# One table sets the order of every engine up to the third token group, in a recurrent attention followed by a gated MLP

## The chip, the cores and the metric

The kernel runs on one core of a Trainium2 chip. A core has a matrix engine (TensorE, PE in the profile), a vector engine (VectorE, DVE), a scalar engine (ScalarE, ACT), GpSimd (POOL) and SyncE (SP), which here only issues transfers. Each engine works through its own queue in order. The metric is the time of one execution in microseconds on the device; lower is better.

## The reference

For each of 4 batches and 8 heads a recurrence runs over 768 positions with head dimension 48. Its output, 3072 tokens of 384 features, goes through a gated MLP with 1536 hidden features.

```python
for t in range(S):
    kt, vt, rt, wt = k[:, :, t], v[:, :, t], r[:, :, t], w[:, :, t]
    cur = np.einsum('bhd,bhe->bhde', u[None] * kt, vt)
    y[:, :, t] = np.einsum('bhd,bhde->bhe', rt, state + cur)
    state = wt[:, :, :, None] * state + np.einsum('bhd,bhe->bhde', kt, vt)
x = y.transpose(0, 2, 1, 3).reshape(B * S, H * D)
g = x @ w_gate
out = (g * (1 / (1 + np.exp(-g))) * (x @ w_val)) @ w_out      # w_*: float64
```

r, k, v, w and u are float32; the three weight matrices arrive as float64.

## The kernel before

**Chunks.** The recurrence is done in 24 chunks of 128 positions, six for each batch, all eight heads at once (four pairs of heads, the halves of a pair on partitions 0 to 47 and 64 to 111). For a chunk n, VectorE scans the decays backwards (`qt`, L192), takes the reciprocal of the whole chunk's decay (L196, L197), multiplies k by it (`kq`, L198), scans forwards (`et`, L201) and multiplies r (L202). From k, r and u in natural order it makes the diagonal term `a0` (L211 to L214), which ScalarE spreads over an identity (`at`, L231). TensorE turns k around (`kb`, L239), multiplies the scores (`sc`, L253); VectorE puts the scores below the diagonal into `at` by a mask (L255). TensorE then forms the chunk's state (`dl`, L272; added to the decayed old state by VectorE, `st` and `sp`) and the output `y` (L301), which ScalarE and VectorE split into an upper half `xh` and a remainder `xl` (L308, L309). In the code a chunk is three steps of a generator, each followed by a third of the preparation of chunk n+1.

**Groups.** The 24 chunks are the tokens of seven groups of 4, 2, 4, 4, 4, 4 and 2 chunks. For a group the MLP runs over twelve blocks f of hidden features: two halves `gv` of nine matmuls each (gate and value; three products of halves for each of three slices of x, L385), SiLU on ScalarE (`sg`, L392), the product on VectorE (L393), its upper half and remainder (`hh` L395, `hl` L397), and the output product `po` (L406), which is issued one block late. After the last block ScalarE copies the output out of PSUM (`ob`, L417) and SyncE stores it.

**Weights.** Block f's weights come as pairs of 32-bit words and are converted once, during the start and group 0: two passes on ScalarE (L150, L152), three on VectorE (L154, L155, L157), the upper half on ScalarE (L158) and the remainder on VectorE (L159). Two blocks' raw weights fit at a time; the load of block f+2 is issued when block f is converted.

**Buffers.** PSUM's eight banks are two buffers for `kb`, `sc`, `dl` and `y` (the pool psA), two for `gv`, four for `po`. In SBUF two buffers take turns for each of the loads `kr` (k and r), `ws` (decays) and `vt` (v), one for `nat`; chunks 2 and 3 keep their kr in buffers that later hold group 1's x.

**Order.** TensorE's instructions run in the order in which the code lists them: the start (chunks 0 to 3, with spin matmuls on a constant between the steps), and then the groups' blocks, with the next group's chunk steps between them at fixed blocks (`at_block`). The transfers of the start are in the code's order too. Everything else on VectorE, ScalarE and SyncE is ordered by the scheduler of the framework. In group 0 the conversion of block f+2 is held behind the one before it.

Of the kernel before, what the change touches and what calls it, by code (L numbers as in the profile page):

```python
# [9 lines left out]
F32 = mybir.dt.float32  # L10
F32R = mybir.dt.float32r
# [25 lines left out]
PEND_MIN = 1e-15  # L37

# [10 lines left out]
def recurrence_then_glu_kernel(  # L49
# [30 lines left out]
    xs, raws, masked = {}, {}, [None]  # L80
# [53 lines left out]
    w_l = cpool.tile([P, NF, 3, DM], F32R, tag="w_l", name="w_l")  # L134

    def load_weights(f):
        raw = wst.tile([P, 3, DM, 2], I32, tag="raw", name=f"raw_{f}")
        for i, src in enumerate((gv_d[f, 0], gv_d[f, 1], wo_d[f])):
            queue(nc.sync.dma_start(raw[:, i].rearrange("p c t -> p (c t)"), src.bitcast(I32)))
        return raw  # L140

    def convert(f):

        raw = raws.pop(f)
        top, low = raw[:, :, :, 1], raw[:, :, :, 0]
        hi, lo = w_h[:, f], w_l[:, f]


        tf, tu = top.bitcast(F32), top.bitcast(U32)
        nc.scalar.activation(tf, tf, AF.Copy, scale=2.0**-112)  # L150

        nc.scalar.activation(low, low.bitcast(U32), AF.Copy, scale=2.0**-29)  # L152
        s = wst.tile([P, 3, DM], U32, tag="s", name=f"s_{f}", bufs=1)
        nc.vector.tensor_scalar(s, tu, 0x1FFFFFFF, 3, ALU.bitwise_and, ALU.logical_shift_left)  # L154
# [3 lines left out]
        nc.scalar.activation(hi, af, AF.Copy)  # L158
        last = nc.vector.tensor_tensor(lo, af, hi.bitcast(F32), ALU.subtract)  # L159
# [5 lines left out]
    wss, krs, nats, vts = {}, {}, {}, {}

    def load_ws(n):
        wss[n] = ld.tile([PR, L + 1], F32, tag="ws", name=f"ws_{n}")
        queue(nc.sync.dma_start(wss[n], wt_d[n]))

    def load_kr(n):

        pool, tag = {2: (mp, "xh"), 3: (mp, "xl")}.get(n, (ld, "kr"))
        krs[n] = pool.tile([PR, 2, NPR, C], F32, tag=tag, name=f"kr_{n}")
        queue(nc.sync.dma_start(krs[n], kr_d[n]))

    def load_nat(n):
        nats[n] = ld.tile([P, 2, H, D], F32, tag="nat", name=f"nat_{n}", bufs=1)
        queue(nc.sync.dma_start(nats[n], nat_d[n]))

    def load_vt(n):
        vts[n] = ld.tile([P, H, D], F32, tag="vt", name=f"vt_{n}")
        queue(nc.sync.dma_start(vts[n], v_d[n]))

    state = [None]

    def prepare(n):

        ws, kr, vt = wss.pop(n), krs[n], vts[n]
        kq, re = kr[:, 0], kr[:, 1]  # L190
        qt = ap_.tile([PR, NPR, C + 1], F32, tag="qt", name=f"qt_{n}", bufs=1)
        nc.vector.tensor_tensor_scan(  # L192
            _flat(qt)[:, ::-1], ws[:, 1:][:, ::-1], _flat(d1q)[:, ::-1], 0.0, ALU.mult, ALU.add
        )
        nc.scalar.activation(pend[:, n, :], qt[:, :, 0], AF.Copy)
        nc.vector.tensor_scalar(d1e[:, :, 0], qt[:, :, 0], PEND_MIN, None, ALU.max)  # L196
        nc.vector.reciprocal(d1e[:, :, 0], d1e[:, :, 0])  # L197
        nc.vector.tensor_tensor(kq, kq, qt[:, :, 1:], ALU.mult)  # L198
# [12 lines left out]
        nc.vector.tensor_tensor(ru, ru, u_bc, ALU.mult)  # L211
        nc.vector.tensor_tensor(ru, ru, nat[:, 0], ALU.mult)
        a0 = ap_.tile([P, H], F32, tag="a0", name=f"a0_{n}")
        nc.vector.tensor_reduce(a0, ru, AX.X, ALU.add)  # L214
        if n + 1 < NC:
            load_nat(n + 1)

        vz = vzs[n % 2]
        vp = vt.rearrange("s (p j) e -> s p j e", j=2)
        nc.scalar.activation(vz[:, :, 0, : D - 32], vp[:, :, 0, 32:], AF.Copy)  # L220
        nc.scalar.activation(vz[:, :, 1, D - 32 :], vp[:, :, 1, : 64 - D], AF.Copy)
        yield a0, vz

    def diagonals(n, a0):

        at = []
        for j in range(2):
            a = ap_.tile([P, NPR, C], F32, tag="at", name=f"at_{n}_{j}", bufs=3)
            for p in range(NPR):
                h = 2 * p + j  # L230
                nc.scalar.activation(a[:, p, :], ident, AF.Copy, scale=a0[:, h : h + 1])  # L231
# [12 lines left out]
    def scores(n, kq, re, at):

        c = n % NCH
        sc = [psA.tile([P, NPR, C], F32, tag="pa", name=f"sc_{n}_{j}") for j in range(2)]
        for p in range(NPR):
            for j in range(2):
                o = slice(64 * j, 64 * j + D)  # L250
                for m in range(2):
                    ms = slice(64 * m, 64 * m + 64)
                    pin(nc.tensor.matmul(sc[j][ms, p, :], kq[o, p, ms], re[o, p, :], start=True, stop=True))  # L253
        for j in range(2):
            masked[0] = nc.vector.copy_predicated(at[j], mask4, sc[j])  # L255
# [353 lines left out]
```

## Time and profile before

| | |
|---|---|
| median of 3 runs | 627.27 us (623.29 to 627.89) |
| the profiled execution | 626.31 us |
| its span, first to last instruction | 624.6 us |
| TensorE, VectorE, ScalarE busy | 579.5, 356.1, 265.5 us |
| mean granted clock of TensorE | 0.972 |
| first product of group 0, 1, 2 | 60.91, 164.41, 224.78 us |
| last matmul of the last group ends | 617.4 us |

A row of the timeline has the start (us from the span's start), the duration, engine, line, operation, tile written <- tiles read, and in brackets the idle time of the engine before it and what ended that. A row of the stages has the stretch, its length, each engine's busy time with its count of instructions, the granted clock of TensorE (1.00 is full), the busy share of the DMA engines and GB/s. A group of instructions by line has its count, the busy time, the mean ns of one, and the idle time before them with what ended most of it. L numbers are lines of the kernel before.

### The profile page before, as it was taken

How to read it: one execution, taken by the hardware profiler on the slowest of the kernel's cores; microseconds unless marked ns; L12 is line 12 of the kernel's file. 1: busy time of each engine (PE TensorE's matmuls, PEld its weight loads, DVE VectorE, ACT ScalarE, POOL GpSimd, SP SyncE). 2: the span in 40 equal slices, each digit the busy share in tenths (PEclk: the TensorE clock that was granted, in tenths of full speed). 3: DMA queues.
4: the chain of work that ended last, by engine and by line, in shares of the span. 5: the costliest groups of instructions: out<-in, count | busy, mean ns of one | idle time of the engine just before them, and what ended most of it. 6: DMA issues, size and time to landing. Idle time of an engine off the chain costs nothing.

```text
span 624.6 us, 12577 instructions
## 1 busy us (share of the span) xinstructions
PE 579.5 (93%) x5330; PEld 501.0 (80%) x5330; DVE 356.1 (57%) x595; ACT 265.5 (43%) x609; POOL 1.9 (0%) x11
## 2 busy tenths in 40 slices
PE   7688999476989989999999999999999999999995
PEld 5477788364889978888888888888888888888994
DVE  7984789978567766365456556545644533132221
ACT  5646666743544444334345333443533432121321
POOL 1000000000000000000000000000000000000000
PEclk9888999979989999999999999999999999999998
DMA  9646453423332233211212212221210110000100
GB/s 276 196 149 181 168 173 126 167 84 95 93 96 83 85 108 83 68 45 54 70 67 83 69 23 76 84 85 50 84 43 1 43 51 2 1 1 0 52 1 30
DMA packets 21903, 50.67 MB, mean 81 GB/s; under 512 B 2513, under 2 KB 8785, under 8 KB 21841
## 3 DMA queue, kind: packets, MB, share of 16 engines
q1 hardware_dynamic: 21840, 49.81, 25.6%
q8 instruction: 44, 0.72, 0.5%
q14 instruction: 19, 0.15, 0.1%
HBM read 45.08 MB, written 4.72 MB: 80 GB/s over the span
## 4 chain that ended last, share of the span: by engine, by line
PE 71%; DVE 10%; DMA 8%; ACT 5%; issue 3%; SPq 1%; DVEq 0%; ACTq 0%
PE gv L385 40%; PE po L406 21%; DMA raw<-in_wo_dram 5%; PE y L301 5%; PE sc L253 3%; DMA vt<-in_vn_dram 2%; DVE qt L192 2%; ACT w_h L158 1%; DVE s L155 1%; PE dl L272 1%; ACT raw L152 1%; DVE s L157 1%; DVE et L201 1%; PE kb L239 1%; ACT at L231 1%
## 5 line engine op out<-in xcount | busy, mean ns | idle before, releaser
L385 PE MATMUL gv<-xh,w_h 128*128 128x512 f32 (+1 forms) x504 | 184.1, 365 | 3.1 <-DVE sg L393 1.8
L385 PE MATMUL gv<-xh,w_l 128*128 128x512 f32 (+1 forms) x504 | 181.6, 360 | 1.0 <-DVE w_l L159 1.0
L385 PE MATMUL gv<-xl,w_h 128*128 128x512 f32 (+1 forms) x504 | 182.2, 361 | 0.0
L393 DVE TENSOR_TENSOR sg<-sg,gv 128x512 f32<-128x512 f32 (+1 forms) x84 | 51.0, 607 | 146.4 <-PE gv L385 145.0
L385 PEld LDWEIGHTS gv<-xh,w_h 128*128 128x128 f32 x504 | 95.0, 189 | 17.6 <-DVE sg L393 3.0
L385 PEld LDWEIGHTS gv<-xl,w_h 128*128 128x128 f32 x504 | 95.0, 188 | 15.3
L385 PEld LDWEIGHTS gv<-xh,w_l 128*128 128x128 f32 x504 | 95.0, 189 | 14.1 <-DVE w_l L159 1.3
L406 PE MATMUL po<-w_h,hh 128*128 128x384 f32 x288 | 101.1, 351 | 0.5 <-ACT hh L395 0.5
L406 PE MATMUL po<-w_h,hl 128*128 128x384 f32 x288 | 97.7, 339 | 2.4 <-DVE hl L397 2.4
L406 PE MATMUL po<-w_l,hh 128*128 128x384 f32 x288 | 97.3, 338 | 0.0
L395 ACT ACTIVATE hh<-sg 128x512 fp32r<-128x512 f32 (+1 forms) x84 | 47.8, 569 | 110.1 <-DVE sg L393 110.1
L392 ACT ACTIVATE sg<-gv 128x512 f32<-128x512 f32 (+1 forms) x84 | 44.7, 533 | 111.8 <-PE gv L385 106.5
L397 DVE TENSOR_TENSOR hl<-sg,hh 128x512 fp32r<-128x512 f32 (+1 forms) x84 | 51.6, 614 | 36.6 <-ACT hh L395 36.0
L231 ACT ACTIVATE at<-ident,a 128x128 f32<-128x128 f32 x192 | 60.7, 390 | 14.3 <-PE y L301 9.3
L406 PEld LDWEIGHTS po<-w_h,hh 128*128 128x128 f32 x288 | 54.3, 189 | 9.0 <-issue 6.0
L406 PEld LDWEIGHTS po<-w_h,hl 128*128 128x128 f32 x288 | 54.3, 189 | 4.6 <-DVE hl L397 3.2
L406 PEld LDWEIGHTS po<-w_l,hh 128*128 128x128 f32 x288 | 54.4, 189 | 0.0
L255 DVE COPY_PREDICATED at<-mask,sc 128x512 f32<-128x512 uint32 x48 | 32.5, 728 | 8.1 <-PE sc L253 8.1
L253 PE MATMUL sc<-kr 48*64 48x128 f32 x768 | 30.8, 279 | 6.9 <-DVE xl L309 3.8
L253 PEld LDWEIGHTS sc<-kr 48*64 48x64 f32 x768 | 22.8, 134 | 15.5 <-issue 4.9
L198 DVE TENSOR_TENSOR kr<-kr,qt 112x512 f32<-112x512 f32 x24 | 16.5, 689 | 29.7 <-DMA kr<-in_kr_dram 29.7
L204 ACT ACTIVATE ws<-ws 112x517 f32<-112x517 f32 x24 | 15.3, 636 | 42.8 <-DVE et L201 42.7
(64 smaller groups left out, 564.0 us busy)
## 6 DMA issues: line engine op xcount, KB each, us to landing
kr<-in_kr_dram SPq DMA_DIRECT2D x24, 448.0 KB, 4.0
nat<-in_nat_dram SPq DMA_DIRECT2D x24, 384.0 KB, 3.1
raw<-in_gv_dram SPq DMA_DIRECT2D x24, 384.0 KB, 4.0
ws<-in_wt_dram SPq DMA_DIRECT2D x24, 226.2 KB, 2.6
vt<-in_vn_dram SPq DMA_DIRECT2D x24, 192.0 KB, 3.5
raw<-in_wo_dram SPq DMA_DIRECT2D x12, 384.0 KB, 4.8
out_dram<-ob SPq DMA_DIRECT2D x24, 192.0 KB, 1.8
u_bc<-in_u_dram SPq DMA_DIRECT2D x1, 192.0 KB, 4.8
```

The source lines that it names most:

```text
L198: nc.vector.tensor_tensor(kq, kq, qt[:, :, 1:], ALU.mult)
L204: nc.scalar.activation(ws, ws, AF.Square)
L231: nc.scalar.activation(a[:, p, :], ident, AF.Copy, scale=a0[:, h : h + 1])
L253: pin(nc.tensor.matmul(sc[j][ms, p, :], kq[o, p, ms], re[o, p, :], start=True, stop=True))
L255: masked[0] = nc.vector.copy_predicated(at[j], mask4, sc[j])
L301: pin(nc.tensor.matmul(y[32 * g : 32 * g + 32, b // 4, :], lhs, rhs, start=first[g] == i, stop=last[g] == i,))
L385: pin(nc.tensor.matmul(gv, a[:, f, j, q * P : (q + 1) * P], x[:, q, :], start=m == 0, stop=m == 3 * NK - 1,))
L392: nc.scalar.activation(sg, ps[0], AF.Silu)
L393: nc.vector.tensor_tensor(sg, sg, ps[1], ALU.mult)
L395: nc.scalar.activation(hh, sg, AF.Copy)
L397: nc.vector.tensor_tensor(hl, sg, hh.bitcast(F32), ALU.subtract)
L406: pin(nc.tensor.matmul(po[j], a[:, ts], x[:, f, 2, :], start=f == 0 and i == 0, stop=f == NF - 1 and i == 2,))
```

## The change

The code of the start and of groups 0 and 1, with all chunk steps up to the output of chunk 9 (the last of group 2), is now one table of some 700 entries. Each entry names a step and its indices (`pred:4:0` is the mask of chunk 4's even heads, `gv:0:2:1` the value half of block 2 of group 0, `spin:22` that many spin matmuls). The code walks the table and calls the steps; while it does so, the instructions of VectorE, ScalarE, TensorE and the transfers all keep the table's order on their engines. From group 2 on the blocks and chunk steps follow as before by `at_block`, and the scheduler orders VectorE, ScalarE and SyncE as before. What else differs:

- the scores of chunks 0 to 3 are in the four banks of `po`, no more in psA; from chunk 4 on they are in psA;
- a SiLU of one element on ScalarE at the very start, so that its table of functions is loaded there and not in group 0;
- the shared 16 columns of v are copied to a padded tile by one ScalarE instruction for a chunk, no more by two;
- the reciprocal of the chunk's decay is taken without the maximum before it (L196); a chunk for which that matters is sent to the fallback by the same test as before;
- 223 spin matmuls in place of 216;
- from group 2 on, the output product `po` stands behind the chunk's `kb`, no more ahead of it, in three of a group's blocks.

```diff
+FREE = 2
+ORDER = """
+spin:25 ws:0 nat:0 ub:0 kr:0 ws:1 raw:0 scan:0 vt:0 seed:0 kr:1 whole:0 raw:1 ru:0 ruk:0 vt:1 a0:0
...
+hh:1:11 hl:1:11
+"""
...
+    def keep(ins):
+        if early[0]:
+            tc.keep_in_program_order(ins)
...
+    nc.scalar.activation(warm, warm, AF.Silu)
...
+    def seed(n):
+        keep(nc.vector.reciprocal(d1e[:, :, 0], qts[n][:, :, 0]))
...
-        nc.scalar.activation(vz[:, :, 0, : D - 32], vp[:, :, 0, 32:], AF.Copy)
-        nc.scalar.activation(vz[:, :, 1, D - 32 :], vp[:, :, 1, : 64 - D], AF.Copy)
+        keep(nc.scalar.activation(z[:, :, ::2, :], shared.rearrange("s p (j e) -> s p j e", j=2), AF.Copy))
...
-        sc = [psA.tile([P, NPR, C], F32, tag="pa", name=f"sc_{n}_{j}") for j in range(2)]
+        if n < first:
+            scs[n] = [psM.tile([P, NPR, C], F32, tag="po", name=f"sc_{n}_{j}", bufs=4) for j in range(2)]
+        else:
+            scs[n] = [psA.tile([P, NPR, C], F32, tag="pa", name=f"sc_{n}_{j}") for j in range(2)]
...
+    for item in ORDER.split():
+        name, *at = item.split(":")
+        ops[name](*map(int, at))
     early[0] = False
...
+    for g in range(FREE, len(GROUPS)):
         steps = 3 * GROUPS[g + 1] if g + 1 < len(GROUPS) else 0
         at_block = [k * (NF - 1) // steps for k in range(steps)]
...
         for f in range(NF):
+            block(g, f)
+            for k in range(at_block.count(f)):
+                if k == 0 and f == 0:
+                    behind()
+                    waiting = None
+                next(attention)
+            if waiting:
+                behind()
+            waiting = (g, f)
```

**Chunk 4's scores on TensorE.** Before (sc_4 are the scores, dl_4 the state products, y_4 the output of chunk 4; gv_0_8_1 is the value half of block 8 of group 0):

```order
L385 MATMUL gv_0_8_1_1278<-xl_0_176,w_h_100 128x512
L253 MATMUL sc_4_0_1295<-kr_4_632 64x128 x2
L253 MATMUL sc_4_1_1296<-kr_4_632 64x128 x2
...
L272 MATMUL dl_4_1324<-vt_4_634,kn_4_1242 32x48
L272 MATMUL dl_4_1324<-vt_4_634,kn_4_1242 16x48
...
L301 MATMUL y_4_1344<-kr_4_632,sp_89 32x128 x12
```

and now:

```order
L483 MATMUL gv_0_2_1_963<-xl_0_319,w_h_103 128x512
L338 MATMUL sc_4_0_983<-kr_4_325 64x128 x2
L338 MATMUL sc_4_1_984<-kr_4_325 64x128 x2
...
L517 MATMUL po_0_0_918<-w_h_103,hh_0_1_974 128x384
...
L483 MATMUL gv_0_3_0_1022<-xh_0_318,w_h_103 128x512
...
L483 MATMUL gv_0_3_1_1037<-xh_0_318,w_h_103 128x512
...
L483 MATMUL gv_0_4_0_1083<-xh_0_318,w_h_103 128x512
...
L358 MATMUL dl_4_1100<-vt_4_691,kn_4_907 32x48
```

The scores moved from block 8 to block 2, and between them and the state products now stand two output products and three halves of the MLP.

**The mask of chunk 4 on VectorE**, with what stands ahead of it. Before (s_10 and w_l_101 belong to the conversion of block 10, qt_5 to chunk 5's preparation, at_4 is the masked tile):

```order
L397 TENSOR_TENSOR hl_0_8_1293<-sg_0_8_1288,hh_0_8_1291 128x512
L154 TENSOR_SCALAR s_10_1262<-raw_10_1143 128x1152
L196 TENSOR_SCALAR d1e_87<-qt_5_1254 112x4
L198 TENSOR_TENSOR kr_5_794<-kr_5_794,qt_5_1254 112x512
L155 SCALAR_TENSOR_TENSOR s_10_1262<-raw_10_1143,s_10_1262 128x1152
L197 RECIPROCAL d1e_87<-d1e_87 112x4
L157 ISA s_10_1262<-raw_10_1143,s_10_1262 128x2304
L159 TENSOR_TENSOR w_l_101<-s_10_1262,w_h_100 128x1152
L255 COPY_PREDICATED at_4_0_1244<-mask_81,sc_4_0_1295 128x512
L255 COPY_PREDICATED at_4_1_1249<-mask_81,sc_4_1_1296 128x512
```

and now:

```order
L282 TENSOR_TENSOR kr_4_325<-kr_4_325,et_4_847 112x512
L295 TENSOR_TENSOR nat_5_939<-nat_5_939 128x384
L221 TENSOR_TENSOR w_l_104<-s_4_911,w_h_103 128x1152
L505 TENSOR_TENSOR hl_0_1_1001<-sg_0_1_913,hh_0_1_974 128x512
L207 TENSOR_SCALAR s_5_1003<-raw_5_868 128x1152
L343 COPY_PREDICATED at_4_0_934<-mask_81,sc_4_0_983 128x512
L211 SCALAR_TENSOR_TENSOR s_5_1003<-raw_5_868,s_5_1003 128x1152
L495 TENSOR_TENSOR sg_0_2_1005<-sg_0_2_1005,gv_0_2_1_963 128x512
```

The mask stands inside a conversion, one step of it ahead, and the mask of the other half comes later (behind hl_0_4, in the conversion of block 7).

**The end of group 1 on VectorE.** st_9, sp_89 and xl_2 belong to chunk 9, kr_11 and et_11 to chunk 11's preparation, sg_1_* and hl_1_* to the last blocks of group 1. Before:

```order
L393 TENSOR_TENSOR sg_1_10_2367<-sg_1_10_2367,gv_1_10_1_2357 128x256
L281 TENSOR_TENSOR st_9_2391<-dl_9_2374,sp_89 48x192 x2
L397 TENSOR_TENSOR hl_1_10_2372<-sg_1_10_2367,hh_1_10_2370 128x256
L260 TENSOR_TENSOR sp_89<-st_9_2391,pend_99 48x4x48 x2
L214 TENSOR_REDUCE a0_12_2862<-nat_12_2655 128x8
L198 TENSOR_TENSOR kr_11_2425<-kr_11_2425,qt_11_2534 112x512
L309 TENSOR_TENSOR xl_2_1664<-y_9_2394,xh_2_1663 128x3x128
L201 SCALAR_TENSOR_TENSOR et_11_2562<-ws_11_2125,d1e_87 112x516
L393 TENSOR_TENSOR sg_1_11_2463<-sg_1_11_2463,gv_1_11_1_2453 128x256
```

and now:

```order
L495 TENSOR_TENSOR sg_1_7_2260<-sg_1_7_2260,gv_1_7_1_2262 128x256
L369 TENSOR_TENSOR st_9_2319<-dl_9_2272,sp_89 48x192 x2
L505 TENSOR_TENSOR hl_1_7_2324<-sg_1_7_2260,hh_1_7_2322 128x256
L349 TENSOR_TENSOR sp_89<-st_9_2319,pend_102 48x4x48 x2
L299 TENSOR_REDUCE a0_12_2847<-nat_12_2642 128x8
L271 TENSOR_TENSOR kr_11_2333<-kr_11_2333,qt_11_2520 112x512
L408 TENSOR_TENSOR xl_2_1735<-y_9_2290,xh_2_1734 128x3x128
L276 SCALAR_TENSOR_TENSOR et_11_2547<-ws_11_2116,d1e_87 112x516
L495 TENSOR_TENSOR sg_1_8_2358<-sg_1_8_2358,gv_1_8_1_2348 128x256
```

The same sequence now stands between blocks 7 and 8, so that the last four blocks of group 1 run behind the last chunk step.

On SP's queue the start's transfers are now ws_0, nat_0, u_bc, kr_0, ws_1, the three of raw_0, vt_0, kr_1, the three of raw_1; before they were ws_0, kr_0, nat_0, u_bc, vt_0, ws_1, kr_1, vt_1 and then raw_0.

More of the change, by code (lines that the diff above doesn't have):

```diff
@@ L165, in recurrence_then_glu_kernel @@
[L165 to L177 removed]
+            keep(nc.sync.dma_start(raws[f][:, i].rearrange("p c t -> p (c t)"), src.bitcast(I32)))
@@ L400, in output, with prepare, attention_steps @@
-    def output(po, f, hh, hl, name):
-        for j in range(len(po)):
+    def prepare(n):
+        for op in (scan, whole, seed, kq):
+            op(n)
+        yield
+        for op in (scan2, re, check):
+            op(n)
+        if n + 2 < NC:
+            ws(n + 2)
+        yield
+        for op in (ru, ruk, a0):
+            op(n)
+        if n + 1 < NC:
+            nat(n + 1)
+        vz(n)
+        yield
+    def attention_steps(start):
+        for n in range(start, NC):
+            c = n % NCH
+            ahead = prepare(n + 1) if n + 1 < NC else iter([0] * 3)
+            if c < NCH - 1:
+                kb(n)
+                kn(n)
+            for j in range(2):
+                diag(n, j)
+            next(ahead)
+            yield
+            sc(n)
+            for j in range(2):
+                pred(n, j)
+            if c > 0:
+                spb(n)
+            next(ahead)
+            yield
+            if c < NCH - 1:
+                dl(n)
+                st(n)
+            y(n)
+            xh(n)
+            xl(n)
+            if n + 2 < NC:
+                kr(n + 2)
+                vt(n + 2)
+            next(ahead)
+            yield
@@ new lines, in recurrence_then_glu_kernel, with gv @@
+    gvs, sgs, hhs, hls, pos = {}, {}, {}, {}, {}
+    def gv(g, f, j):
+        x_h, x_l = xs[g]
+        nt = x_h.shape[2]
+        ps = psM.tile([P, nt], F32, tag="gv", name=f"gv_{g}_{f}_{j}", bufs=2)
+        m = 0
+        for q in range(NK):
+            for a, x in ((w_h, x_h), (w_l, x_h), (w_h, x_l)):
+                pin(nc.tensor.matmul(
+                    ps, a[:, f, j, q * P : (q + 1) * P], x[:, q, :], start=m == 0, stop=m == 3 * NK - 1,
+                ))
+                m += 1
+        gvs[g, f, j] = ps
@@ L428, in spin @@
         for _ in range(times):
-            pin(nc.tensor.matmul(idle, mask.bitcast(mybir.dt.bfloat16)[:, :P], busy, start=True, stop=True))
-    spin(24)
-    for k in range(3 * GROUPS[0]):
-        if k == 3 * GROUPS[0] - 4:
-            convert(0)
-        elif k == 3 * GROUPS[0] - 1:
-            convert(1)
-        next(attention)
-        spin(16)
-    early[0] = False
-    behind = masked[0].ins
-    waiting = None
-    t0 = 0
-    for g, tiles in enumerate(GROUPS):
-        xh, xl = xs.pop(g)
-        po = [None] * tiles
+            pin(nc.tensor.matmul(idle, busy[:, :P], busy, start=True, stop=True))
```

484 lines of the change are left out of this document (248 added, 236 removed).

## The prediction

> **What bounds the kernel now.** I read the chain of waits first, then the span cut into its stages (start, group 0, group 1, groups 2 to 6), then TensorE's rows wherever it stood idle, then the DMA-fed waits of VectorE.
>
> ```profile
> PE 71%; DVE 10%; DMA 8%; ACT 5%; issue 3%; SPq 1%; DVEq 0%; ACTq 0%
> core 0: us, PE busy (x) PEld busy (x) DVE busy (x) ACT busy (x) POOL busy (x), PEclk, DMA share, GB/s
> 0.00:60.91 60.91, 46.57 (x688) 36.69 (x689) 46.76 (x78) 34.06 (x78) 1.94 (x11) 0.89 0.67 201
> 60.91:164.40 103.49, 84.45 (x563) 71.61 (x561) 87.75 (x117) 60.98 (x105) 0.00 (x0) 0.93 0.41 133
> 164.40:224.80 60.40, 57.11 (x768) 52.99 (x767) 40.22 (x82) 29.46 (x89) 0.00 (x0) 0.97 0.31 96
> 224.80:617.40 392.60, 391.31 (x3316) 339.72 (x3316) 180.84 (x319) 140.95 (x340) 0.00 (x0) 1.00 0.15 47
> ```
>
> From 224.80 us on, the first product of group 2, TensorE is busy 391.31 of 392.60 us at full clock and VectorE not half the time: a new order gains nothing there. All that can be won lies ahead. The same view for the spin matmuls alone gives
>
> ```profile
> 0.00:60.91 60.91, 30.00 (x216) 22.42 (x216) 0.89 0.67 201
> ```
>
> so 16.6 us of the start's 46.57 on TensorE compute anything; the start is paced by VectorE (46.76) and what it waits for. In groups 0 and 1 TensorE is idle 19.04 + 3.29 = 22.3 us of 163.9. The five longest gaps (TensorE's timeline; the bracket is the idle time before the row and what ended it) make 19.0 of that:
>
> ```profile
> 128.87 0.86 PE L272 MATMUL dl<-vt,kn 128*32 128x48 f32 x32 [11.12 <-DVE at L255]
> 144.90 0.51 PE L385 MATMUL gv<-xh,w_h 128*128 128x512 f32 x1 [1.30 <-DVE sg L393]
> 152.35 0.91 PE L301 MATMUL y<-kr,sp 112*32 112x128 f32 x24 [4.06 <-DVE at L255]
> 180.15 0.54 PE L406 MATMUL po<-w_h,hl 128*128 128x384 f32 x1 [1.33 <-DVE hl L397]
> 224.78 0.50 PE L385 MATMUL gv<-xh,w_h 128*128 128x512 f32 x1 [1.19 <-ACT sg L392]
> ```
>
> The 11.12 is chunk 4: its scores stand ahead of two weight conversions that the masking on VectorE (L255) stands behind. Gaps cost twice. Cut along the clock's steps, the span around three of them reads
>
> ```profile
> 125.73:129.15 3.42, 0.28 (x16) 0.28 (x20) 2.32 (x3) 1.06 (x1) 0.00 (x0) 0.50 0.00 0
> 129.15:132.56 3.41, 3.34 (x81) 3.02 (x73) 3.35 (x7) 1.18 (x2) 0.00 (x0) 0.50 0.02 5
> 153.04:156.45 3.41, 3.41 (x43) 2.56 (x35) 1.59 (x3) 1.36 (x5) 0.00 (x0) 0.50 0.76 233
> 176.93:180.35 3.42, 1.70 (x11) 1.44 (x12) 3.36 (x8) 3.36 (x10) 0.00 (x0) 1.00 0.18 33
> 180.35:183.76 3.41, 3.41 (x15) 3.31 (x15) 2.01 (x7) 2.50 (x10) 0.00 (x0) 0.50 0.39 147
> ```
>
> TensorE works 0.28 + 3.34 + 3.41 + 3.41 = 10.4 us at clock 0.50, which is 5.2 us lost. Without gaps and half clock, groups 0 and 1 take 163.9 - 22.3 - 5.2 = **136.4 us** of TensorE. The row at 176.93 shows what starts it: 1.72 us idle in 3.42, and the next 3.4 us run at 0.50. The Trainium skill (TensorE: Matmul & The Clock Gate, section "Why this matters for your kernels") allows gaps up to about 3 us between bursts; this trace disagrees at 1.7.
>
> **The change, part by part.**
>
> *Start (before 57 us).* VectorE's work ahead of group 0's first product changes as the table says: chunk 4's first scan, reciprocal and product, the last step of conversion 2 and the first of conversion 3 now come ahead of it; four of the 112x4 maxima go.
>
> ```profile
> L192 DVE TENSOR_TENSOR_SCAN qt<-ws,d1q 112x516 f32<-112x516 f32 x24 | 29.5, 1228 | 2.3 <-DMA ws<-in_wt_dram 2.1
> L198 DVE TENSOR_TENSOR kr<-kr,qt 112x512 f32<-112x512 f32 x24 | 16.5, 689 | 29.7 <-DMA kr<-in_kr_dram 29.7
> L159 DVE TENSOR_TENSOR w_l<-s,w_h 128x1152 fp32r<-128x1152 f32 x12 | 16.3, 1358 | 9.5 <-ACT w_h L158 9.3
> L154 DVE TENSOR_SCALAR s<-raw 128x1152 uint32<-128x1152 uint32 x12 | 9.0, 752 | 0.0
> L197 DVE RECIPROCAL d1e<-d1e 112x4 f32<-112x4 f32 x24 | 4.3, 179 | 0.5
> L196 DVE TENSOR_SCALAR d1e<-qt 112x4 f32<-112x4 f32 x24 | 4.0, 166 | 0.1
> 3.81 1.23 DVE L192 TENSOR_TENSOR_SCAN qt<-ws,d1q 112x516 f32<-112x516 f32 x1 [1.75 <-DMA ws<-in_wt_dram]
> 52.01 0.56 DVE L309 TENSOR_TENSOR xl<-y,xh 128x384 fp32r<-128x384 f32 x1 [5.24 <-ACT xh L308]
> 48.05 1.27 ACT L150 ACTIVATE raw<-raw 128x1152 f32<-128x1152 f32 x1 [3.23 <-DMA raw<-in_wo_dram]
> ```
>
> 46.76 + 1.23 + 0.18 + 0.69 + 1.36 + 0.75 - 4 x 0.17 = 50.3 us, of which about 1.0 are memsets before 3.81 us, when the first data lands. Never idle, VectorE is through at 3.8 + 49.3 = 53.1. Before, it waited: 5.24 us in one piece, because ScalarE's queue stood 3.23 on a weight load ahead of the copy that VectorE needed. With the third load issued right behind the first conversion, and the scores out of the two-buffer pool, where they waited for the previous chunk's xl to give up a buffer,
>
> ```profile
> PE sc L253 <- DVE xl L309: 3.8, 3, 1.9
> raw<-in_gv_dram SPq DMA_DIRECT2D x24, 384.0 KB, 4.0
> 0.00:20.00 20.00, 14.95 (x186) 11.69 (x187) 16.39 (x31) 11.22 (x27) 1.94 (x11) 1.00 0.94 299
> ```
>
> (3.8 us in three waits), I take 4 us of waits: group 0 starts at **57** instead of 60.9. Bounds: 53.6 with almost none, and at the start's old density, 46.76 in 57.1 us, 3.8 + 49.3/0.82 = 64. On SP's queue the three transfers of raw_0, 1152 KB, now stand ahead of kr_1; at the 299 GB/s of the first 20 us (the row's last figure) kr_1 lands 3.9 us later. VectorE wants it later too, behind chunk 0's masks, its state copy and a conversion step; if that covers nothing the 3.9 are the 4 that I allow.
>
> *Groups 0 and 1.* The table lets score products, masks and state products stand blocks apart on TensorE, with products of the GLU between, and spreads ten conversions between chunks. What VectorE must do up to 224.80 is 46.76 + 87.75 + 40.22 = 174.7, less 12 x 0.17 and the memsets 171.7; from 3.8 on that ends at 175.5 at best. TensorE needs 57 + 136.4 = 193.4. So TensorE sets the floor, with VectorE 91% full beside it, and ScalarE (124.5) far from it. Not all waits go. One is in the order: near the end of group 1, kq_11 waits for kr_11, which is loaded only when y_9 has read that buffer, and xl_9, the scan et_11 and sg_1_8 queue behind it on VectorE. The nearest case:
>
> ```profile
> 205.25 1.28 ACT L231 ACTIVATE at<-ident,a 128x128 f32<-128x128 f32 x4 [0.87 <-PE y L301]
> 208.12 0.69 DVE L198 TENSOR_TENSOR kr<-kr,qt 112x512 f32<-112x512 f32 x1 [1.00 <-DMA kr<-in_kr_dram]
> 220.24 0.28 PE L385 MATMUL gv<-xh,w_h 128*128 128x256 f32 x1
> 222.36 0.34 PE L406 MATMUL po<-w_h,hh 128*128 128x384 f32 x1
> 217.26 0.42 DVE L393 TENSOR_TENSOR sg<-sg,gv 128x256 f32<-128x256 f32 x1 [0.61 <-PE gv L385]
> ```
>
> From the end of y to kq's start 2.9 us, then 0.69 + 0.56 + 1.23 + 0.42 until sg is done: 5.8. TensorE holds one output product and three halves of 1.06 each (2.12 for two): 4.2. So 1.6 us idle. Beyond it I grant one half-clocked stretch (1.7) and 2.3 us of short waits where an sg stands behind a conversion step of 1.36: together 5.6, bounds 0 and, from VectorE's density, the first rival. By the page on the clock, none of these gaps would slow TensorE and the sum would be 1.7 us less; by the row at 176.93 it stands. Group 2 starts at 57 + 136.4 + 5.6 = **199 us** instead of 224.8.
>
> *ScalarE's table.* The second load stood at
>
> ```profile
> 61.97 1.28 ACT L392 ACT_TABLE_LOAD   x1
> 63.27 0.60 ACT L392 ACTIVATE sg<-gv 128x512 f32<-128x512 f32 x1
> 66.32 0.68 DVE L393 TENSOR_TENSOR sg<-sg,gv 128x512 f32<-128x512 f32 x1
> ```
>
> and SiLU, over at 63.9, was read only at 66.32, when VectorE had ended a conversion step: the load is hidden and its going is worth 0, at most 1.3. The Trainium skill (ScalarE: Activation LUTs, section "What ACT_TABLE_LOAD costs") puts a switch at about 2.66 us with its drain; here SiLU begins 0.02 after the load's end, so 1.28 is all.
>
> *Groups 2 on.* Same instructions; the transposes kb move one output product earlier at three blocks of a group, one padded copy of v goes from ScalarE and one maximum from VectorE, both hidden under TensorE. 0, with 1 us either way.
>
> Sum: 224.8 - 199 = 25.8 us. Span 624.6 - 25.8 = 598.8; the profiled execution itself took 626.31, 1.7 over its span, so 600.5. The median of the runs before, 627.27, is 1 above it: **601**.
>
> **Rivals.** *VectorE's density stays.* In group 0 it was busy 87.75 of 103.49, 85%, and its waits came from ScalarE and DMA, which the table orders but doesn't shorten. Then its work ends at 3.8 + 171.7/0.85 = 206, time 608. Against it: 9.3 us of VectorE's waits were for upper halves that ScalarE did late (L159's row), which an order can mend.
>
> *The order only moves the gaps* (no change). The load of kr for chunk n+2 still waits for y of chunk n; if each of chunks 5 to 11 holds VectorE's head as long as the worst before,
>
> ```profile
> 174.99 0.69 DVE L198 TENSOR_TENSOR kr<-kr,qt 112x512 f32<-112x512 f32 x1 [2.85 <-DMA kr<-in_kr_dram]
> ```
>
> that is 7 x 2.85 = 20 us, and three half-clocked stretches more: 199 + 20 to 25, time 621 to 626. For most chunks the table has other VectorE work between release and use, which speaks against it.
>
> *Slower: the clock.* With every queue frozen, two engines that miss each other by 2 us stop TensorE until it is at clock 0.50 again. A stretch of 3.4 us with 1.9 idle followed by one at half clock loses 3.6. The loss removed (27.5) and the start (3.9) are used up, and 1% more, at (31.4 + 6.3)/3.6, ten such pairs of the 20 that fit into groups 0 and 1; with twelve, 57 + 136.4 + 43 = 236.4, time 639. What speaks for it: 176.93 shows how little idle it takes. Against it, with conversions beside the products:
>
> ```profile
> 80.00:100.00 20.00, 20.00 (x98) 17.47 (x97) 16.31 (x18) 13.59 (x15) 0.00 (x0) 1.00 0.38 123
> ```
>
> TensorE full, VectorE 82%, clock 1.00.
>
> **Numbers.** Forecast 0.66, VectorE's density 0.17, moved gaps 0.09, slower 0.08. Low end: 53.6 + 136.4 + 1.6 = 191.6, time 593, less the 3 us by which the fastest run lay under the profiled one: 590. High end 617, between the density rival and the moved gaps. About 1% is what can be told from no change: faster 0.83, same 0.09, slower 0.08.
>
> **What would show it.** Right: group 0's first product at 54 to 60 us and group 2's at 194 to 204; no gap over 2 us on TensorE between them but the one behind kr_11; VectorE about 90% busy up to there; at most two half-clocked stretches; 392 to 394 us from group 2's first product to the last matmul. Wrong: VectorE below 85% with waits on DMA; the start over 62; PEclk under 0.95 in group 0.

## The result

| | before | after |
|---|---|---|
| median | 625.55 us (623.29 to 627.89, 4 runs) | 600.54 us (598.86 to 603.18, 4 runs) |
| the profiled execution and its span | 626.31, 624.6 us | 603.18, 601.5 us |
| first product of group 0, 1, 2 | 60.91, 164.41, 224.78 us | 55.8, 142.0, 203.0 us |
| mean granted clock of TensorE | 0.972 | 0.993 |

The ratio is 0.9604, with a 95% interval of 0.9546 to 0.9661: the changed kernel is 25 us, 4%, faster. (The text on the change speaks of some 700 entries in the table; it has 574. The prediction took 627.27 us, the median of three runs, for the kernel before; with the fourth run it is 625.55.)

The stages of the kernel after, in the columns of the prediction's first view (stretch, its length, busy time of PE, PEld, DVE, ACT and POOL with counts, granted clock, DMA share, GB/s):

```profile
0.00:55.80 55.80, 43.56 (x695) 34.53 (x696) 48.43 (x77) 34.82 (x75) 1.84 (x11) 0.97 0.83 235
55.80:142.00 86.20, 84.73 (x668) 71.07 (x665) 83.80 (x113) 61.59 (x109) 0.00 (x0) 1.00 0.48 156
142.00:203.00 61.00, 54.17 (x665) 49.59 (x663) 41.15 (x81) 27.73 (x78) 0.00 (x0) 0.97 0.30 91
203.00:595.10 392.10, 390.91 (x3318) 339.31 (x3316) 176.11 (x302) 138.88 (x324) 0.00 (x0) 1.00 0.15 46
```

Of the 23.1 us between the two spans the start gives 5.1 and group 0 gives 17.3 (103.5 to 86.2). Group 1 gives nothing: 61.0 us, 60.4 before. Groups 2 to 6 take 392.1 instead of 392.6 us, and the tail behind the last matmul 6.4 instead of 7.2. In group 0 two engines are now nearly full: TensorE is busy 84.73 and VectorE 83.80 of 86.20 us.

What TensorE waits for has changed. Its longest waits by tile (us in total, times, the longest), groups 0 and 1, of the kernel before:

```profile
PE dl L272 <- DVE at L255: 11.1, 1, 11.1
PE y L301 <- DVE at L255: 4.1, 1, 4.1
PE po L406 <- DVE hl L397: 2.4, 2, 1.3
```

and of the kernel after:

```profile
PE gv L483 <- ACT sg L492: 5.3, 4, 1.9
PE gv L483 <- DVE sg L495: 0.9, 2, 0.5
PE po L517 <- DVE hl L505: 0.6, 2, 0.4
PE dl L358 <- DVE at L343: 0.2, 1, 0.2
```

The 15.2 us behind VectorE's masks are 0.2. The largest part of what is left, 5.3 us, stands behind SiLU on ScalarE, nearly all of it in group 1. VectorE's own wait in group 0, for the upper halves of the weights on ScalarE, of before and then of after:

```profile
DVE w_l L159 <- ACT w_h L158: 8.4, 8, 2.4
```

```profile
DVE w_l L221 <- ACT w_h L218: 1.6, 3, 0.9
```

### The profile page after: what moved, and what is told of

Its sections match the earlier page's. It is cut to its first block, busy times and chain, and to the rows that moved or that the text cites. A ratio compares the mean times of both kernels' runs of the same rounds, so it can differ in the third digit from the quotient of the medians.

```text
span 601.5 us, 12520 instructions
## 1 busy us (share of the span) xinstructions
PE 573.4 (95%) x5337; PEld 494.5 (82%) x5337; DVE 350.0 (58%) x572; ACT 263.0 (44%) x585; POOL 1.8 (0%) x11
## 4 chain that ended last, share of the span: by engine, by line
PE 72%; DVE 11%; DMA 8%; ACT 5%; issue 2%; SPq 1%; DVEq 0%; ACTq 0%
PE gv L483 42%; PE po L517 22%; PE y L394 4%; DMA kr<-in_kr_dram 2%; PE sc L338 2%; DMA ws<-in_wt_dram 2%; DMA raw<-in_wo_dram 2%; DVE et L276 1%; PE dl L358 1%; ACT at L306 1%; DVE s L211 1%; DMA vt<-in_vn_dram 1%; DVE at L343 1%; DVE s L215 1%; DVE qt L259 1%
## 5 line engine op out<-in xcount | busy, mean ns | idle before, releaser
L546 PE MATMUL idle<-mask 128*128 128x256 bf16 x223 | 29.1, 290 | 2.5 <-POOL mask L154 2.5
L338 PE MATMUL sc<-kr 48*64 48x128 f32 x768 | 27.9, 277 | 3.8 <-DVE kr L282 2.2
L338 PEld LDWEIGHTS sc<-kr 48*64 48x64 f32 x768 | 21.4, 133 | 11.7 <-issue 4.9
```

The source lines that it names most:

```text
L338: pin(nc.tensor.matmul(scs[n][j][ms, p, :], krs[n][o, 0, p, ms], krs[n][o, 1, p, :], start=True, stop=True,))
L546: pin(nc.tensor.matmul(idle, busy[:, :P], busy, start=True, stop=True))
```

## The experiments

The ratios are to the kernel before, measured in the same series of runs as each experiment; the changed kernel's is 0.9604 [0.9546, 0.9661]. A theory to be tested stood behind the forecast: the gain is the order's, and it comes because masks, scores and state products no longer stand behind conversions. The rivals: the small edits carry it, or one engine's order alone.

### 1. The small edits alone

The kernel before with these edits of the change (and the single padded copy of v), and the old order:

```diff
+    nc.scalar.activation(warm, warm, AF.Silu)
...
-        nc.vector.tensor_scalar(d1e[:, :, 0], qt[:, :, 0], PEND_MIN, None, ALU.max)
...
+        if n < GROUPS[0]:
+            sc = [psM.tile([P, NPR, C], F32, tag="po", name=f"sc_{n}_{j}", bufs=4) for j in range(2)]
```

> The kernel before with only the small edits of the change (scores of the first four chunks in the output's banks, one load of ScalarE's table, one padded copy of v, no maximum); the order stays the old one. Theory (the gain is the order's): group 0 still starts at 58 to 61 us, the gap of about 11 us ahead of chunk 4's state product stays, and the time is 622 to 626, at most 4 us under the kernel before (the 3.8 us of score waits). Rival (the banks and the table load carry the gain): group 0 starts at 56 to 57 and the time is 600 to 612.

Measured: 626.33 us, ratio 1.0015 [0.9989, 1.0041]. Group 0 starts at 57.8 us, 3.1 earlier, but what the start saves is lost again: TensorE's gap ahead of chunk 4's state product is still 10.67 us, and group 2 starts at 224.9. By themselves, in the old order, the small edits are worth nothing.

### 2. Whose order is it?

In the changed kernel all four engines' instructions are bound to the table. Four variants release one or two of them to the scheduler by taking `keep` (or, for TensorE, `pin`) off its instructions; the transfers keep the table's order in all of them. With both VectorE and ScalarE released:

```diff
-        keep(nc.vector.copy_predicated(ats[n, j], mask4, scs[n][j]))
+        free(nc.vector.copy_predicated(ats[n, j], mask4, scs[n][j]))
...
-        keep(nc.scalar.activation(sgs[g, f], ps, AF.Silu))
+        free(nc.scalar.activation(sgs[g, f], ps, AF.Silu))
```

(and so on for each instruction of the two engines in the table's part; `free` does nothing).

> The changed kernel, with TensorE and the DMA queues still in the table's order, but VectorE and ScalarE left to the scheduler. Theory (the order on VectorE is what counts, since the masks stood behind conversions there): most of the gain goes, group 0 and 1 take 155 to 170 us instead of 147, time 609 to 626. Rival (the order on TensorE alone is enough, the other engines follow by their waits): 600 to 604, with groups 0 and 1 within 2 us of 147.

Measured: 627.67 us, ratio 1.0043 [1.0007, 1.0080]. With TensorE and the transfers alone in the table's order the whole gain is gone. Two of TensorE's waits in groups 0 and 1 of this run:

```profile
PE gv L486 <- ACT sg L495: 8.0, 5, 2.0
PE dl L361 <- DVE at L346: 1.4, 1, 1.4
```

So TensorE's order alone does take the masks' wait out of groups 0 and 1 (1.4 us, 15.2 before), but nothing is gained by it. SiLU is waited for instead, and in the start the masks' wait grows from 5.5 to 10.6 us, so that group 0 begins at 67.3 us (60.9 in the kernel before). Then one of the two engines was released at a time, ScalarE alone:

> The changed kernel with TensorE, the DMA queues and VectorE in the table's order, and ScalarE alone left to the scheduler. With VectorE and ScalarE both left to it the whole gain was gone (628). Theory (VectorE's order carries the gain, since it is the engine that is full): 600 to 608. Rival (ScalarE's order carries it, since VectorE waited 9.3 us for upper halves and 5.2 us for a copy of ScalarE's): 618 to 630, with VectorE under 90% busy in group 0.

and VectorE alone:

> The changed kernel with TensorE, the DMA queues and ScalarE in the table's order, and VectorE alone left to the scheduler. Theory (VectorE's order carries the gain): 618 to 630, with masks behind conversion steps again and gaps over 2 us on TensorE. Rival (ScalarE's order carries it): 600 to 608.

Measured: 620.79 us, ratio 0.9932 [0.9912, 0.9951], with ScalarE released; 626.04, ratio 1.0004 [0.9975, 1.0033], with VectorE released. Each time the forecast came in that put the gain down to the released engine (618 to 630 in both runs), so neither engine carries it alone: without ScalarE's order VectorE's is worth 0.7%, about 4 us, and without VectorE's order ScalarE's is worth nothing. Group 0 begins at 62.4 us with ScalarE released and at 65.1 with VectorE released (55.8 in the changed kernel); the rest is lost in groups 0 and 1, which take 156.8 and 160.6 us instead of 147.2. The rows at the start of group 0 show one wait of several in each. With ScalarE released (timeline of ScalarE, then VectorE, then TensorE):

```profile
59.62 1.21 ACT L205 ACTIVATE raw<-raw 128x1152 int32<-128x1152 uint32 x1 [3.89 <-DMA raw<-in_wo_dram]
60.73 1.20 ACT L200 ACTIVATE raw<-raw 128x1152 f32<-128x1152 f32 x1
61.83 0.47 ACT L406 ACTIVATE xh<-y 128x384 fp32r<-128x384 f32 x1
...
62.34 0.56 DVE L411 TENSOR_TENSOR xl<-y,xh 128x384 fp32r<-128x384 f32 x1 [3.98 <-ACT xh L406]
...
62.35 0.50 PE L486 MATMUL gv<-xh,w_h 128*128 128x512 f32 x1 [3.43 <-ACT xh L406]
```

The scheduler put two conversion passes, the first of which waits 3.89 us for its weights, ahead of the copy `xh` that group 0's first product needs; VectorE, in the table's order, then stands still with it. With VectorE released, at the first product of group 0 that reads the remainder `xl` (VectorE, then TensorE):

```profile
65.41 1.35 DVE L214 SCALAR_TENSOR_TENSOR s<-raw,s 128x1152 uint32<-128x1152 uint32 x1
66.68 1.23 DVE L262 TENSOR_TENSOR_SCAN qt<-ws,d1q 112x516 f32<-112x516 f32 x1
67.82 0.71 DVE L352 TENSOR_TENSOR sp<-st,pend 48x192 f32<-48x192 f32 x2
68.56 1.36 DVE L218 CUSTOM_DVE_ANT_0 s<-raw,s 128x2304 uint16<-128x2304 uint16 x1
69.95 0.56 DVE L411 TENSOR_TENSOR xl<-y,xh 128x384 fp32r<-128x384 f32 x1
...
70.57 0.80 PE L486 MATMUL gv<-xl,w_h 128*128 128x512 f32 x1 [4.80 <-DVE xl L411]
```

Conversions, a scan and a state step are served first and TensorE waits 4.80 us. It is the same kind of wait as the prediction's gap of 11.12 us, at another step: work that nobody waits for yet stands ahead of the one instruction that TensorE waits for. Last, TensorE itself was released, VectorE and ScalarE bound:

```diff
     def pin(ins):
-        if straight[0]:
+        if straight[0] and not early[0]:
             tc.keep_in_program_order(ins)
```

> The changed kernel with VectorE, ScalarE and the DMA queues in the table's order, and TensorE left to the scheduler up to group 2. Theory (TensorE's order must match the others', because its queue is served in order and a score product ahead of the GLU's products holds them all): 615 to 640. Rival (with VectorE, the full engine, in the table's order TensorE's own order hardly matters): 600 to 606.

Measured: 602.82 us, ratio 0.9647 [0.9622, 0.9673]. The rival was right: binding TensorE is worth 2.3 us by the medians, and the intervals of the two ratios overlap. In the profiled run groups 0 and 1 take 146.7 us against 147.2. TensorE's order is another one in this run: chunk 4's state products start at 76.16 us and are cut in two by an output product, where the changed kernel has them in one piece at 84.67. But chunk 4's scores stay early, at 70.31 us (72.36 in the changed kernel). So where VectorE and ScalarE are bound, the scheduler finds an order for TensorE that does nearly as well; what TensorE's old order would cost beside them is not shown. How much the transfers' order carries was not tried by itself. Nor was the table without the scores in the output's banks: as the code reads, the scores in the two-buffer pool and what must free those buffers would then wait for each other in a circle.

### 3. What sets group 0's length?

> The changed kernel with group 0's gate and value products left without their third part (72 products with xl, 16.5 us of TensorE's work at the 0.229 us that one takes); the computation lacks that part. VectorE's work stays. Theory (in group 0 VectorE and TensorE are both full, 83.8 and 84.7 of 86.2 us): group 0 gets at most 4 us shorter, since VectorE sets the same floor, and the time is 596 to 600. Rival (TensorE alone is the floor and VectorE is only kept busy by the order): 10 to 16 us shorter, 584 to 590.

```diff
-            for a, x in ((w_h, x_h), (w_l, x_h), (w_h, x_l)):
+            for a, x in ((w_h, x_h), (w_l, x_h), (w_h, x_l))[: 2 if g == 0 else 3]:
...
```

Measured: 604.01 us, ratio 0.9655 [0.9619, 0.9692], above both forecasts. Group 0 of this kernel:

```profile
54.70:139.70 85.00, 73.34 (x595) 60.24 (x593) 81.88 (x109) 60.08 (x105) 0.00 (x0) 0.96 0.48 154
```

With 11.4 us less busy time on TensorE (73.34 against 84.73) the stage is only 1.2 us shorter, within the theory's 4. VectorE is 96% busy: it is a floor of its own, nearly as high as TensorE's. TensorE also spent 6.8 us of this stage at half clock, in two stretches behind new gaps, which it did not in the changed kernel; but VectorE is idle for 3.1 us of the stage, so without them it could have been shorter by about that at most. In the whole time nothing of the 1.2 us is seen, since group 1, in which TensorE ran 6.8 us at half clock from 190.9 us on, took 63.2 us here (61.0 in the changed kernel).

### 4. What is left in group 1

The longest gap after the change, in TensorE's timeline and then ScalarE's:

```profile
151.95 0.38 PE L483 MATMUL gv<-xh,w_h 128*128 128x256 f32 x1 [1.88 <-ACT sg L492]
```

```profile
151.03 0.49 ACT L533 ACTIVATE ob<-po 128x384 f32<-128x384 f32 x1 [2.01 <-DMA out_dram<-ob]
151.42 0.20 ACT L264 ACTIVATE pend<-qt 112x4 f32<-112x4 f32 x1
151.52 0.38 ACT L492 ACTIVATE sg<-gv 128x256 f32<-128x256 f32 x1
```

Group 0's third output copy waits 2.01 us until a store has emptied one of its two buffers, and SiLU stands behind it. Two entries of the table were moved, `ob:0:1` behind `hh:1:1` and `ob:0:2` behind `silu:1:2`:

```diff
-hl:1:0 gv:1:1:1 ob:0:1 seed:9 whole:9 a0:9 silu:1:1 ob:0:2 pred:7:1 nat:10 gv:1:2:0 sg:1:1 hh:1:1
-gv:1:2:1 hl:1:1 silu:1:2 dl:7
+hl:1:0 gv:1:1:1 seed:9 whole:9 a0:9 silu:1:1 pred:7:1 nat:10 gv:1:2:0 sg:1:1 hh:1:1 ob:0:1
+gv:1:2:1 hl:1:1 silu:1:2 ob:0:2 dl:7
```

> The changed kernel with two of group 0's output copies on ScalarE moved behind later GLU steps, so that the first SiLUs of group 1 no longer stand behind a copy that waits for a store. Theory (the 1.88 us gap at 150 us and the half-clocked stretch behind it come from that copy): the gap and the stretch go, 1.9 to 3.6 us faster than the changed kernel, 597 to 599. Rival (another wait takes its place, or the copies delay the output products of group 1): within 1 us of the changed kernel.

Measured: 599.58 us, ratio 0.9565 [0.9513, 0.9618]; the gap and the half-clocked stretch are gone, group 1 takes 58.5 us. By the medians that is 1.0 us, where the rival had at most 1, by the ratios 2.4, where the theory had 1.9 to 3.6; the intervals overlap, so the size was open until the last run of this part. Then the wait near 190 us, on VectorE, ScalarE and TensorE of the changed kernel:

```profile
189.73 0.69 DVE L271 TENSOR_TENSOR kr<-kr,qt 112x512 f32<-112x512 f32 x1 [1.75 <-DMA kr<-in_kr_dram]
```

```profile
190.24 0.31 ACT L313 ACTIVATE vz<-vt 128x128 f32<-128x128 f32 x1 [1.30 <-DMA vt<-in_vn_dram]
190.46 0.37 ACT L492 ACTIVATE sg<-gv 128x256 f32<-128x256 f32 x1
```

```profile
190.88 0.38 PE L483 MATMUL gv<-xh,w_h 128*128 128x256 f32 x1 [1.24 <-ACT sg L492]
192.52 0.39 PE L483 MATMUL gv<-xh,w_h 128*128 128x256 f32 x1 [0.32 <-DVE sg L495]
195.53 0.39 PE L483 MATMUL gv<-xh,w_h 128*128 128x256 f32 x1 [1.67 <-ACT sg L492]
```

Both engines wait for chunk 11's loads with the MLP's steps behind. The first cure, with the output copies moved as above, gave those loads buffers of their own:

```diff
+            if n == first + 7:
+                spare = wst.tile([P, 3, DM, 2], I32, tag="raw", name=f"kr_{n}")
...
```

> The changed kernel with the two output copies moved as in the run before (group 1's SiLUs no longer behind a copy that waits for a store), and the last chunk's loads of k, r and v put into weight buffers that are free by then, so that they need not wait for the state product two chunks earlier. Theory (the waits that I undersized in group 1 are these two): group 1 takes 54 to 56 us instead of 61.0 (58.5 with the first edit alone), the gaps of 1.24 and 1.7 us near its end go, and the time is 594 to 597. Rival (something else, VectorE's queue or the recurrence itself, is as late there): group 1 stays at 58 us and the time at 599 to 600.

Measured: 601.78 us, ratio 0.9614 [0.9589, 0.9638]: nothing gained and above both forecasts; group 1 takes 60.0 us. VectorE's timeline shows two waits in place of one:

```profile
181.43 0.69 DVE L280 TENSOR_TENSOR kr<-kr,qt 112x512 f32<-112x512 f32 x1 [1.11 <-DMA kr<-in_kr_dram]
...
189.10 0.69 DVE L280 TENSOR_TENSOR kr<-kr,qt 112x512 f32<-112x512 f32 x1 [1.12 <-DMA kr<-in_kr_dram]
```

The first is chunk 11's, which now stands ahead of block 7's `sg`: its load needs no state product any more, but goes out at 177.34, right behind the load of decays ahead of it in SyncE's queue, and is waited for all the same. The second is chunk 12's `kq`, which has moved up to the place where chunk 11's had been, ahead of `xl` and block 8's `sg`. Neither is in the table, whose preparation ends with chunk 10. The scheduler places them, and it is free to place them between entries of the table. So the second cure leaves the loads alone, keeps the moved copies, and binds chunk 11's preparation, and chunk 10's own steps around it, where the code lists them, behind group 1 and the first block of group 2:

```diff
+                early[0] = g == FREE and taken[0] < 3
                 next(attention)
+                early[0] = False
+                taken[0] += 1
```

> The changed kernel with the two output copies moved as before, and chunk 11's steps (its scans, products and copies, which the table doesn't list) kept by program order behind group 1's and the first block of group 2, so that the scheduler can no longer put them into the end of group 1. Theory (the gaps of 1.24 to 1.7 us near 190 us come from the scheduler's placing of chunk 11, and of chunk 12 where chunk 11 was cured, ahead of the GLU's steps): those gaps go, group 1 takes 54 to 56 us instead of 58.5, group 2 starts at 195 to 197, 594 to 597 in all. Rival (that work is only put off, and delays chunk 11's scores in group 2): the time stays at 599 to 600, with as much idle in group 2 as group 1 has lost.

Measured: 592.61 us (591.77 to 593.09), ratio 0.9471 [0.9443, 0.9498], better than the theory's 594 to 597. Its stages:

```profile
53.80:139.90 86.10, 84.50 (x666) 71.08 (x664) 83.68 (x113) 61.58 (x109) 0.00 (x0) 1.00 0.48 156
139.90:191.20 51.30, 51.05 (x666) 48.03 (x665) 31.80 (x64) 22.57 (x60) 0.00 (x0) 1.00 0.29 89
191.20:583.90 392.70, 391.34 (x3318) 339.28 (x3316) 185.91 (x319) 143.60 (x342) 0.00 (x0) 1.00 0.16 49
```

Group 1 takes 51.3 us with 0.25 us idle. VectorE does 17 instructions less in it and as many more later (319 against 302 in the changed kernel), where they cost 0.6 us (392.7 against 392.1). This version beats both kernels: 8 us under the changed one, with ratio intervals that do not overlap, and 5% under the kernel before. Last, the same without the moved output copies:

> The changed kernel with only chunk 11's steps kept behind group 1 (which together with the two moved output copies gave 592.6); the output copies of group 0 stay where the table has them. Theory (the copy that waits for a store costs its 1.88 us gap and the half-clocked stretch behind it, 1.7 us, whatever comes later): 594.5 to 596.5, with the gap near 150 us and one half-clocked stretch in the trace. Rival (the slack that comes with chunk 11 out of the way takes it up): within 1 us of 592.6.

Measured: 595.07 us (594.99 to 595.88), ratio 0.9523 [0.9484, 0.9562]. So by the medians binding chunk 11 is worth 5.5 us by itself (600.54 to 595.07), and the copies 2.5 us behind it (595.07 to 592.61). The times of the three kernels do not overlap from run to run; the intervals of their ratios just touch, so the sizes are good to a microsecond or two. The gap is there (1.83 us, from 149.42 on), but not the half-clocked stretch that was expected behind it; that belongs to the clock, next.

### 5. What lowers the clock

> The changed kernel with a test behind its last group: five stages of twelve bursts of small bf16 products on TensorE, with a pause after each burst while ScalarE copies, the pauses growing from stage to stage. It adds work of its own and its time isn't compared. Theory (from the stretch of 3.42 us with 1.72 idle that was followed by one at half clock): windows of 3.4 us in which TensorE was busy under about 0.55 are followed by a window at clock 0.50, windows over 0.60 are not, also where no single pause reaches 3 us. Rival (only a single pause of 3 us or more lowers the clock): the stages with pauses of 1 to 2.5 us stay at clock 1.00.

The clock of each trace changes only at the ends of windows of 3.41 us, at a fixed spacing. Some windows of this test, each followed by its next one (behind the stretch's length, TensorE's busy time; the clock is the sixth figure behind the comma, the counts in brackets aside, 1.00 or 0.50):

```profile
787.17:790.58 3.41, 1.72 (x16) 1.30 (x15) 0.00 (x0) 1.48 (x3) 0.00 (x0) 1.00 0.00 0
790.58:794.00 3.42, 3.42 (x33) 3.06 (x32) 0.00 (x0) 0.00 (x0) 0.00 (x0) 1.00 0.02 5
794.00:797.41 3.41, 1.44 (x14) 1.06 (x12) 0.00 (x0) 1.48 (x3) 0.00 (x0) 1.00 0.01 2
797.41:800.82 3.41, 3.41 (x18) 2.43 (x17) 0.00 (x0) 0.00 (x0) 0.00 (x0) 0.50 0.00 0
```

A window half idle stays without effect here, and so it went seven times, every second window from 746 to 791 us; at 1.43 to 1.44 us busy the next window was once at 0.50 (the row at 794.00) and once at 1.00 (a window at 892.98 us, not shown). In the last stage every pause lasts 3.01 us, and only its place differs. The first pause shown here is shared by two windows, the second lies almost whole in one:

```profile
913.46:916.88 3.42, 2.16 (x20) 1.69 (x18) 0.00 (x0) 1.13 (x2) 0.00 (x0) 1.00 0.02 5
916.88:920.29 3.41, 1.66 (x16) 1.49 (x17) 0.00 (x0) 1.64 (x3) 0.00 (x0) 1.00 0.00 0
920.29:923.70 3.41, 3.32 (x31) 2.72 (x28) 0.00 (x0) 0.00 (x0) 0.00 (x0) 1.00 0.00 0
923.70:927.12 3.42, 0.50 (x5) 0.46 (x6) 0.00 (x0) 2.77 (x4) 0.00 (x0) 1.00 0.00 0
927.12:930.53 3.41, 3.41 (x19) 2.43 (x17) 0.00 (x0) 0.00 (x0) 0.00 (x0) 0.50 0.00 0
```

The shared pause left the clock at 1.00, as did its three repetitions; with 0.50 us busy (four times) the next window was always at 0.50. So the theory's mechanism holds (the idle share of a fixed window of 3.41 us counts, and pauses of 2 us can be enough) and its threshold was put too high for this work: about 0.42 of the window here. The rival, a single pause of 3 us, falls both ways: 2 us were enough at 794.00, and 3 us were not where two windows shared them. In the kernels the line is not sharp: the 0.50 of the prediction's row was enough, 0.56 was enough at 184.70 us of the version with the spare buffers (1.91 of 3.41), and 0.51 was not at 193.6 us of the changed kernel, though the same window of the test's run, also at 0.51, was followed by half clock. What besides the busy share counts was not settled.

What the window decides shows in two runs with the same gap, the changed kernel (1.88 us) and then the one with only chunk 11 bound (1.83 us):

```profile
149.20:152.62 3.42, 1.54 (x13) 1.34 (x12) 1.81 (x5) 1.48 (x5) 0.00 (x0) 1.00 0.52 195
152.62:156.03 3.41, 3.41 (x41) 3.19 (x43) 0.73 (x2) 0.56 (x2) 0.00 (x0) 0.50 0.59 207
```

```profile
146.95:150.36 3.41, 2.47 (x20) 2.26 (x19) 2.96 (x6) 1.41 (x6) 0.00 (x0) 1.00 0.54 181
150.36:153.78 3.42, 2.53 (x38) 2.40 (x41) 0.88 (x3) 2.02 (x6) 0.00 (x0) 1.00 0.48 157
```

In the first the gap lies in one window and 3.4 us at half clock follow; in the second it is shared by two and costs only itself. The Trainium skill (TensorE: Matmul & The Clock Gate, section "What's actually happening") says that the window of 3413 ns runs freely, so that where work falls in it differs from run to run; the windows here agree, since they begin at 5.5, 5.8 and 7.0 us of three spans. The same page of the Trainium skill, section "HAM oscillation — how this bites in real kernels", bars idle gaps over about 3.4 us; the rows at 794.00 and 149.20, with pauses of 2 us and under, differ.

### 6. ScalarE's table

```diff
-    nc.scalar.activation(warm, warm, AF.Silu)
```

> The changed kernel without the early SiLU on one element, so that ScalarE's table is loaded twice again. Theory (the load is hidden): the time stays within 1 us of the changed kernel's. Rival (VectorE and TensorE are now both full in group 0, so that SiLU is on the path): 1.3 us slower or more, to be seen as a gap on TensorE of about 1.3 us near 60 us.

Measured: 604.15 us, ratio 0.9637 [0.9585, 0.9690]. Timeline of ScalarE, VectorE and TensorE near 60 us:

```profile
59.36 1.28 ACT L489 ACT_TABLE_LOAD   x1
60.66 0.60 ACT L489 ACTIVATE sg<-gv 128x512 f32<-128x512 f32 x1
...
61.28 0.69 DVE L492 TENSOR_TENSOR sg<-sg,gv 128x512 f32<-128x512 f32 x1 [0.99 <-ACT sg L489]
...
61.31 0.50 PE L480 MATMUL gv<-xh,w_h 128*128 128x512 f32 x1 [1.72 <-ACT sg L489]
```

The gap is there, 1.72 us against 0.56 at the same place of the changed kernel: in the new order the load is no longer hidden, since VectorE asks for SiLU at once. This is the sign that the rival named. But group 2 starts at 203.0 us in both profiles. The medians stand 3.6 us apart, which is the rival's forecast too, but the intervals of the ratios overlap. What the early load is worth lies between nothing and that and stays open.

## Why the prediction was right, and where it missed

601 us was forecast and 600.5 measured; the profiled execution was put at 600.5 and took 603.18. That the medians agree to 0.5 us is in part luck: group 2 began 4 us later than forecast (203.0 against 199), the groups behind it and the tail gave back 1.3, and the profiled execution, put 0.5 us under the median, was the slowest of the four, 2.6 us over it. Point by point:

- **The start** was put at 57 and is 55.8, with 48.43 us of VectorE's work in it, where the sum had 50.3. In the variants that share this order, group 0 begins at 53.8 to 55.8.
- **The floor of groups 0 and 1**, 136.4 us of TensorE's work, was right: with chunk 11 bound and the copies moved the two take 86.1 + 51.3 = 137.4.
- **The waits beyond it** were the term that was mis-sized: 5.6 us were allowed, and 147.2 - 136.4 = 10.8 came. Nearly all of the difference is in group 1: in the version that reaches the floor group 0 is as long (86.1 against 86.2), group 1 is 51.3 us instead of 61.0. The step that failed reads "So 1.6 us idle", for the wait behind kr_11, with "one half-clocked stretch (1.7) and 2.3 us of short waits" beside it. Near 190 us three gaps came, 1.24 + 0.32 + 1.67 = 3.2, twice the 1.6; the half-clocked stretch came too, but behind another wait, at 152.62 us. The prediction followed VectorE's queue and the load that it waits for, but ScalarE has the same kind of wait (1.30 for `vt`, ahead of SiLU), and the copy that waits for a store (2.01) wasn't seen at all. The step also said of the wait "One is in the order": it isn't in the table but in what the scheduler adds to it, and binding those steps gained more than its gaps (5.5 us). Of the 7.2 us between group 1 in the version with moved copies (58.5, TensorE busy 53.02) and with chunk 11 bound too (51.3, busy 51.05), 5.2 are idle time and 2.0 are busy time of equally many products (666); why these got shorter wasn't traced.
- **Why the order helps.** The prediction gave TensorE the first place: "The table lets score products, masks and state products stand blocks apart on TensorE". The masks' wait did go, 15.2 us to 0.2, but the runs put the cause elsewhere: with TensorE alone in the table's order that wait is 1.4 us in groups 0 and 1 and the time is no better than before. VectorE's and ScalarE's orders are needed together, and TensorE's need not be bound beside them. So the theory that stood ahead of the experiments holds in its first half (the gain is the order's); freeing the masks is only a part of why.
- **ScalarE's table** was costed at nothing, at most 1.3. The reason given, that VectorE reads SiLU late, held only in the old order. The sum was not tested sharply enough to say more.
- **Groups 2 to 6**, costed at nothing: 392.1 against 392.6.
- **The rivals.** VectorE's density rose from 85% to 97% in group 0, so that rival fell by its number there; yet its idea, that VectorE is a floor of its own, is right (third experiment), and the sentence "So TensorE sets the floor, with VectorE 91% full beside it" was too weak for group 0. Moved gaps: VectorE waits for `kr` in two places of group 1, 3.2 us together, and nowhere in group 0, where the rival had seven waits of 2.85 for chunks 5 to 11. Slower by the clock: one half-clocked stretch (152.6 to 156.0 us) where ten were needed for a loss.
- **The signs named**: no gap over 2 us was right (1.88 the longest) and so was at most two half-clocked stretches. The one gap that was excepted, behind kr_11, was not the longest. One sign missed: VectorE was to be about 90% busy up to group 2 and was busy 173.38 of 203.0 us, 85%, since in group 1 it is busy 41.15 of 61.0 (67%); that is close to the 85% below which the forecast was to be wrong.

## What to carry to other kernels

When engines work in order, look at each wait for what is queued behind the waiting instruction, on every engine that feeds the critical one, ScalarE's copies and their stores included; here waits of 1.3 and 2.0 us for a load and a store cost TensorE nearly as much as they lasted (1.24 and 1.88) because SiLU stood behind them. Where VectorE, ScalarE or both were left to the scheduler, an order bound on the other engines was worth nothing to 4 us here. And an order that stops in the middle leaves the scheduler free to place later work between its entries: binding the next chunk's steps, with the instructions unchanged, gave 5.5 us more by the medians. Ask for each stage which engines are full: in group 0 two are, and taking 11 us of busy time from one of them shortened the stage by 1.2.

## What the runs showed of the hardware

The clock falls by the idle share of a fixed window of 3.41 us, and pauses of 2 us can be enough: in the test, 2.0 us idle of 3.41 halved the clock of the next window in two cases of three and 1.7 in none of seven, while in the kernels 1.5 and 1.7 us did so, too (busy 1.91 and 1.70 of 3.41). Pauses of 3.01 us left the clock alone where two windows shared them (busy 2.16 and 1.66 of 3.41) and halved it where one window held nearly all (busy 0.50). So, by the rows, a gap of 1.88 us cost 3.6 in one run (with half of the 3.41 that followed) and one of 1.83 only itself in another, by where it fell.
